# Shared tile's value product and O turn as whole-array products, its stores and remainder loads 64 rows outermost, and the first pair's q and k prepared head by head

## The chip, the cores and the metric

The kernel runs on one core of one Trainium2 chip. The metric is the device time in microseconds (us) of one execution. The kernel before takes 579.23 us (median of 3 runs, 577.52 to 580.37). The profiled execution's span, from its first to its last instruction, is some 1.8 us under the time measured for that execution; starts in the trace are counted from the start of the span.

## The reference, cut to what matters

```python
def _attn_ref(q, k, v, tau):                 # q, k, v: 8 batches, 8 heads, 576 rows, 64 columns
    scale = 1.0 / np.sqrt(q.shape[-1])
    scores = scale * np.matmul(q, k.transpose(0, 1, 3, 2))
    thresh = np.max(scores, axis=-1, keepdims=True) - tau
    scores = np.where(scores >= thresh, scores, -1000000000.0)
    ...                                      # softmax over what is left
    return np.matmul(attn, v)

def _moe_ref(x, w_in, w_out):                # x: 4608 x 512, w_in: 512 x 2048, w_out: 2048 x 512
    h = x @ w_in
    g = h - np.tanh(h)
    return g @ w_out
```

Attention's output, put back as 4608 rows of 512, is the MLP's input.

## The kernel before

It works on 32 pairs of heads, four pairs to a batch. A head has 576 = 4 x 128 + 64 rows, so a pair has nine score tiles of 128 rows: four for each head, and one *shared* tile that holds the 64 rows that are left over from both heads. I number pairs from 1, and follow the kernel by the start of each pair's shared value product. In pairs 1 to 4 there is no MLP work yet. The MLP weights are loaded piece by piece and cast by GpSimd from the start until pair 7. From pair 5 on, the MLP of the batch before is spread between the score tiles. Up to pair 8 the weights of the softmax are transposed on TensorE, later by DMA. kS is a copy of k with the halves swapped. After pair 32 the MLP of the last batch is left, and then that of all shared rows.

The parts that the change touches (cut; `...` marks cuts):

```python
    def split(p, t, fast=False):             # q or k as a sum of two fp16 parts
        ...                                  # fast (first pair): ScalarE and VectorE, all 576 columns at once
            nc.gpsimd.tensor_scalar(out=x, ...)
            nc.gpsimd.tensor_copy(out=hl[:, :, 0, :], in_=x)
            nc.gpsimd.tensor_tensor(out=hl[:, :, 1, :], ...)

    def attend(i):                           # value product
        ...
        if kd == "M":                        # the shared tile
            pt = pts.pop(i)
            for c in range(5):
                n = 64 if c == 4 else P
                for hh in range(2):          # half of the array's columns each
                    nc.tensor.matmul(
                        out=po[64 * hh : 64 * hh + 64, 4, :],
                        lhsT=pt[0:n, c * P + 64 * hh : c * P + 64 * hh + 64],
                        rhs=vb[0:n, hh, c, :], start=(c == 0), stop=(c == 4),
                    )
    ...
    def emit_x(p):                           # O turn: four whole-array transposes, then
        for hh in range(2):                  # the shared block, by quarters of the array
            s = slice(64 * hh, 64 * hh + 64)
            nc.tensor.matmul(out=ps[s, 512:576], lhsT=o[s, 4, 0, :], rhs=ident_bf[s, s], is_transpose=True, ...)
    ...
                rows = out.rearrange("(b s) n -> b s n", b=B)     # store of shared rows: batch outermost
                to = rows[2 * ms : 2 * ms + 2, MB:S, :]
    ...
            if s + AHEAD in w_when:          # every fourth score tile: one weight piece
                if loaded:
                    w_cast()                 # GpSimd, of the piece loaded four tiles ago
                piece = next(pieces, None)
                if piece:
                    w_load(piece)
```

In the traces GpSimd and the loads' queue each work in program order. Two places in these orders will matter: a weight cast stands on GpSimd in front of the next pair's split of k, and a weight load stands on its queue behind the two transfers of kS, a copy of k with the halves swapped, which must wait for VectorE's copy of the turned k (kS issued at 55.58 and 56.16 us, the load at 58.85).

Of the kernel before, what the change touches and what calls it, by code (L numbers as in the profile page):

```python
# [9 lines left out]
F32 = mybir.dt.float32  # L10
# [8 lines left out]
def kernel(  # L19
# [12 lines left out]
    P = 128  # L32
# [58 lines left out]
    for i in range(NM):  # L91
        zm = const.tile([P, 5 * P], BF16, name=f"zm{i}")
        nc.vector.memset(zm[:, S : 5 * P], -STEEP)
        zms.append(zm)

    pool = lambda name, bufs, **kw: ctx.enter_context(
        tc.tile_pool(name=name, bufs=bufs, **kw)
    )
# [18 lines left out]
    ps_y = pool("ps_y", 1, space=PSUM)  # L117

    ctx.enter_context(tc.manual_schedule())
    warm = const.tile([P, 1], F32, name="warm")  # L120
    nc.vector.memset(warm, 0.0)
    nc.scalar.activation(out=warm, in_=warm, func=ACT.Exp)


    raws = {}
# [3 lines left out]
    def load(p, t):  # L129
        b, h0 = p // HPAIR, 2 * (p % HPAIR)  # L130
        hs = slice(h0, h0 + 2)
        src = {"k": k, "q": q, "v": v}[t]
        eng = nc.scalar if p == 0 and t == "q" else nc.sync
        r = raws[p, t] = raw_pool.tile([P, 10, D], F32, name=f"{t}raw", tag=t)
        n = 8 if t == "v" else 10
        eng.dma_start(
            out=r[:, 0:n, :].rearrange("p (h c) d -> p h (c d)", h=2)[:, :, 0 : 4 * D],
            in_=src[b, hs, 0:512, :].rearrange("h (p c) d -> p h (c d)", c=4),
        )
        if t == "v":  # L140
            rem = src[b, hs, 512:S, :].rearrange("h s d -> s h d")
            eng.dma_start(out=r[0:64, 8:10, :], in_=rem)
            eng.dma_start(out=r[64:P, 8:10, :], in_=rem)
        else:
            eng.dma_start(out=r[:, 4, :], in_=src[b, hs, 512:S, :])

    hls = {}

    def split(p, t, fast=False):
        r = raws.pop((p, t))[:, 0:9, :]  # L150
        hl = hl_pool.tile([P, TPP, 2, D], FP16, name=f"{t}hl", tag=t)
        if fast:
            nc.scalar.mul(out=hl[:, :, 0, :], in_=r, mul=QKSC)
            nc.vector.scalar_tensor_tensor(
                out=hl[:, :, 1, :], in0=r, scalar=QKSC, in1=hl[:, :, 0, :],
                op0=ALU.mult, op1=ALU.subtract,
            )
        else:
            x = hl_pool.tile([P, TPP, D], F32, name="xs", tag="xs")
            nc.gpsimd.tensor_scalar(  # L160
                out=x, in0=r, scalar1=QKSC, scalar2=1.0, op0=ALU.mult, op1=ALU.mult
            )
            nc.gpsimd.tensor_copy(out=hl[:, :, 0, :], in_=x)
            nc.gpsimd.tensor_tensor(  # L164
                out=hl[:, :, 1, :], in0=x, in1=hl[:, :, 0, :], op=ALU.subtract
            )
        hls[p, t] = hl

    def split_v(p):
        r, vb = raws.pop((p, "v")), vbs[p % NV]  # L170
# [8 lines left out]

    mats = {}  # L180

    def turn(p, t):
        hl = hls.pop((p, t))
        ps = ps_big.tile([P, W], FP16, name=f"ps_{t}", tag="big")
        for c in range(TPP):
            nc.tensor.matmul(  # L186
                out=ps[:, c * P : (c + 1) * P],
                lhsT=hl[:, c, :, :].rearrange("p a d -> p (a d)"),
                rhs=ident_f16, is_transpose=True, start=True, stop=True,
            )  # L190
        m = qk_pool.tile([P, W], FP16, name=f"{t}T", tag=t)
        nc.vector.tensor_copy(out=m, in_=ps)  # L192
        mats[p, t] = m
        if t == "k" and p == 0:
            ps = ps_big.tile([P, W], FP16, name="ps_ks", tag="big")
            for c in range(TPP):
                for a in range(2):
                    nc.tensor.matmul(
                        out=ps[64 * a : 64 * a + 64, c * P : (c + 1) * P],
                        lhsT=hl[:, c, 1 - a, :],  # L200
                        rhs=ident_f16, is_transpose=True, start=True, stop=True,
                    )
            sw = qk_pool.tile([P, W], FP16, name="kS", tag="ks")
            nc.vector.tensor_copy(out=sw, in_=ps)
            mats[p, "ks"] = sw
        elif t == "k":
            sw = qk_pool.tile([P, W], FP16, name="kS", tag="ks")
            nc.sync.dma_start(out=sw[0:D, :], in_=m[D:P, :])
            nc.sync.dma_start(out=sw[D:P, :], in_=m[0:D, :])
            mats[p, "ks"] = sw  # L210


    MAIN = (slice(0, 512), slice(640, W))
# [101 lines left out]
    def attend(i):  # L315

        p, j = divmod(i, TPP)
        kd, vb = kind(j), vbs[p % NV]
        if kd == "A":
            return  # L320
        if j in (1, 6):
            ops[p, int(j > 4)] = ps_o.tile([P, 5, D + 1], F32, name="psO", tag="o")
        po = ops[p, int(j > 4)]
        if kd == "M":
            pt = pts.pop(i)
            for c in range(5):
                n = 64 if c == 4 else P
                for hh in range(2):
                    nc.tensor.matmul(  # L329
                        out=po[64 * hh : 64 * hh + 64, 4, :],  # L330
                        lhsT=pt[0:n, c * P + 64 * hh : c * P + 64 * hh + 64],
                        rhs=vb[0:n, hh, c, :], start=(c == 0), stop=(c == 4),
                    )
            return
        pt, hh = pts.pop(i), int(j > 4)

        for ab in range(2):
            blocks = [(4 * ab + ab + c, c) for c in range(4)]
            blocks.append((4, 4 + ab))
            for n, (blk, c) in enumerate(blocks):  # L340
                nc.tensor.matmul(  # L341
                    out=po[:, (j - 1 - 5 * hh) + ab, :],
                    lhsT=pt[:, blk * P : (blk + 1) * P], rhs=vb[:, hh, c, :],
                    start=(n == 0), stop=(n == 4),
                )
# [3 lines left out]
    def norm(p, hh):  # L349
        po = ops.pop((p, hh))  # L350
        if hh == 0:
            osb[p] = o_pool.tile([P, 5, 2, D], BF16, name="osb")
        n = 5 - hh
        rc = st_pool.tile([P, 5], F32, name="rc", tag="rc")
        nc.vector.reciprocal(out=rc[:, 0:n], in_=po[:, 0:n, D])
        nc.vector.tensor_tensor(
            out=osb[p][:, 0:n, hh, :], in0=po[:, 0:n, 0:D],
            in1=rc[:, 0:n].unsqueeze(2).to_broadcast([P, n, D]), op=ALU.mult,
        )

    xs = {}

    def emit_x(p):
        o = osb.pop(p)
        ps = ps_h.tile([P, S], BF16, name="psX", tag="h")
        for t in range(4):
            nc.tensor.matmul(
                out=ps[:, t * P : (t + 1) * P],
                lhsT=o[:, t, :, :].rearrange("p a d -> p (a d)"),
                rhs=ident_bf, is_transpose=True, start=True, stop=True,  # L370
            )
        for hh in range(2):
            s = slice(64 * hh, 64 * hh + 64)
            nc.tensor.matmul(
                out=ps[s, 512:576], lhsT=o[s, 4, 0, :], rhs=ident_bf[s, s],
                is_transpose=True, start=True, stop=True,
            )
        b = p // HPAIR
        if p % HPAIR == 0:
            xs[b] = x_pool.tile([P, DM_C, MB], BF16, name="xT")  # L380
        nc.vector.tensor_copy(out=xs[b][:, p % HPAIR, :], in_=ps[:, 0:512])
        nc.vector.tensor_copy(out=xR[:, p % HPAIR, b, :], in_=ps[:, 512:S])


    gs, stores = {}, []
# [29 lines left out]
    def project(m, ms, part, ps, last):  # L415
        for n in range(4 * part, 4 * part + 4):
            nc.tensor.matmul(  # L417
                out=ps, lhsT=gs[m][:, n, ms * P : (ms + 1) * P],
                rhs=w_out_sb[:, n, :], start=(n == 0), stop=(n == DF_C - 1),
            )  # L420
        if part == 3:
            yo = y_pool.tile([P, d_model], F32, name="yo")
            if last:
                nc.scalar.copy(out=yo, in_=ps)
            else:
                nc.vector.tensor_copy(out=yo, in_=ps)  # L426
            if m < B:
                rows = out[m * S : m * S + MB, :].rearrange("(p c) n -> c p n", c=4)
                to = rows[ms]
            else:  # L430
                rows = out.rearrange("(b s) n -> b s n", b=B)
                to = rows[2 * ms : 2 * ms + 2, MB:S, :]
            stores.append(lambda: nc.sync.dma_start(out=to, in_=yo))

    def layers(m, tail):

# [66 lines left out]
        for d, f in PREP[3 if p == 1 else 0 :]:  # L503
            plan.setdefault(first - d, []).append(lambda p=p, f=f: f(p))

    for t in ("k", "q", "v"):
        load(0, t)
    for t in ("k", "q"):
        split(0, t, fast=True)
    for t in ("k", "q"):  # L510
        turn(0, t)
    split_v(0)
    for t in ("k", "q", "v"):
        load(1, t)
# [8 lines left out]
    for s in range(-AHEAD, NTILE + LAG + 3):  # L523
# [7 lines left out]
            shift(s + AHEAD - 1)  # L531
        if 0 <= s + AHEAD < NTILE:
            scores(s + AHEAD)
        if 0 <= s + MASK < NTILE:
            kink(s + MASK)
        bend()
# [79 lines left out]
```

## Time and profile before

| | before |
|---|---|
| time, median (range) | 579.23 us (577.52 to 580.37) |
| span | 576.3 us |
| shared value product of pair 1, 5, 9, 32 | 28.78, 79.96, 138.57, 487.51 us |
| last pair's shared tile to the end | 88.76 us |
| distance of shared tiles deep in the middle | 15.65 us (13.56 for the first pair of a batch) |

The prediction below shows the lines for the bound, the start, the middle and the end. More will be needed: what VectorE pays for normalising one head's tile. The columns are line, engine, operation, tiles, shapes and count; then the busy sum and the mean in ns; then the idle time ahead:

```profile
L356 DVE TENSOR_TENSOR osb<-psO,rc 128x320 bf16<-128x320 f32 x32 | 15.7, 491 | 1.1
L356 DVE TENSOR_TENSOR osb<-psO,rc 128x256 bf16<-128x256 f32 x32 | 13.6, 424 | 1.1
```

Lines in order of time have start, length, operation, and in brackets the idle time before it with what ended it.

```profile
67.34 0.68 PE L186 MATMUL ps_k<-ident_f,khl 128*128 128x128 f16 x9 [1.05 <-POOL khl L164]
```

### The profile page before, as it was taken

What the parts mean: (1) busy time and instruction counts of PE and PEld (TensorE: products, weight loads), DVE (VectorE), ACT (ScalarE), POOL (GpSimd) and SP (SyncE); (2) the same over time, 40 slices, a digit from 0 to 9 for tenths busy, and PEclk for the clock granted to TensorE, in tenths of its full rate; (3) what the DMA queues carried; (4) which work ended last, traced back from release to release, by engine and by line L of the source; (5) the groups of instructions that cost most, each with busy time, mean ns of one, the idle gap of its engine ahead of it and who ended that gap; (6) DMA issues with size and microseconds to landing.
All of it is one profiled execution on the core that took longest, in us unless ns stands there. A gap on an engine that the chain in (4) does not pass through costs nothing.

```text
span 576.3 us, 13882 instructions
## 1 busy us (share of the span) xinstructions
PE 535.3 (93%) x5146; PEld 303.6 (53%) x5146; DVE 442.6 (77%) x1312; ACT 440.1 (76%) x634; POOL 215.6 (37%) x310
## 2 busy tenths in 40 slices
PE   3889899999999999998999999999999999999990
PEld 2566566665555555554555555555555555444440
DVE  3888888888988988888888888888889896444410
ACT  1889898898888898887898988888889888333400
POOL 6646683753433344444444343345333400000000
PEclk9999999999999999999999999999999999999996
DMA  6556755448889999779989999998999865110111
GB/s 180 170 170 175 211 171 160 138 109 176 176 180 183 180 197 197 173 179 185 174 192 182 186 196 178 188 203 189 179 185 176 184 128 120 38 38 36 38 45 46
DMA packets 186923, 89.48 MB, mean 155 GB/s; under 512 B 150632, under 2 KB 175208, under 8 KB 186856
## 3 DMA queue, kind: packets, MB, share of 16 engines
q1 hardware_dynamic: 186454, 88.31, 70.2%
q8 instruction: 40, 0.66, 0.5%
q10 hardware_dynamic: 402, 0.29, 0.2%
q14 instruction: 27, 0.22, 0.1%
HBM read 37.75 MB, written 9.44 MB: 82 GB/s over the span
## 4 chain that ended last, share of the span: by engine, by line
PE 75%; DMA 6%; ACT 6%; DVE 6%; POOL 2%; issue 1%; SPq 1%; ACTq 0%; POOLq 0%; DVEq 0%
PE psY L417 20%; PE psH L391 17%; PE psS L242 17%; PE psO L341 5%; PE ps_k L186 3%; PE psS L232 3%; ACT pT L302 3%; DVE sc L248 3%; DMA kS<-kT 2%; PE psHt L391 2%; PE psZ L293 2%; ACT z L274 2%; PE psO L329 2%; PE ps_q L186 2%; DMA out_dram<-yo 2%
## 5 line engine op out<-in xcount | busy, mean ns | idle before, releaser
L248 DVE TENSOR_SCALAR_CACHE_REDUCE sc<-psS 128x576 f32<-128x576 f32 x288 | 216.4, 751 | 24.4 <-PE psS L232 10.8
L274 ACT ACTIVATE z<-sc,nb 128x576 bf16<-128x576 f32 x256 | 195.5, 768 | 27.2 <-DVE nb L257 26.0
L417 PE MATMUL psY<-w_out_sb,g 128*128 128x512 bf16 x576 | 145.4, 379 | 0.0
L310 ACT ACTIVATE pT<-zT 128x1152 f16<-128x1152 bf16 (+1 forms) x120 | 127.9, 1066 | 11.6 <-DMA zT<-z 11.0
L391 PE MATMUL psH<-xT,w_in_sb 128*128 128x512 bf16 x480 | 123.4, 379 | 0.0
L242 PE MATMUL psS<-kT,qT 128*128 128x512 f16 (+1 forms) x512 | 105.7, 288 | 8.4 <-DVE nb L257 4.7
L242 PEld LDWEIGHTS <-qT 128*128 128x128 f16 x1024 | 74.8, 98 | 70.7 <-issue 12.4
L242 PE MATMUL psS<-kS,qT 128*128 128x512 f16 (+1 forms) x512 | 105.8, 289 | 2.7 <-DMA kS<-kT 2.6
L410 DVE SCALAR_TENSOR_TENSOR g<-th,psH 128x512 bf16<-128x512 f32 x128 | 87.3, 682 | 25.3 <-ACT th L404 25.1
L404 ACT ACTIVATE th<-psH 128x512 f32<-128x512 f32 x128 | 74.5, 582 | 18.6 <-PE psH L391 18.4
L160 POOL TENSOR_SCALAR xs<-kraw 128x576 f32<-128x576 f32 x31 | 20.8, 669 | 165.9 <-DMA kraw<-in_k_dram 120.3
L417 PEld LDWEIGHTS <-g 128*128 128x128 bf16 x576 | 49.6, 98 | 57.7 <-issue 2.5
L391 PEld LDWEIGHTS <-w_in_sb 128*128 128x128 bf16 x576 | 48.9, 98 | 54.2 <-issue 2.7
L341 PEld LDWEIGHTS <-pT 128*128 128x128 f16 x1280 | 55.6, 98 | 24.3 <-ACT pT L310 2.1
L341 PE MATMUL psO<-vb,pT 128*128 128x65 bf16 x1280 | 61.2, 193 | 0.6 <-ACT pT L310 0.6
L302 ACT ACTIVATE pT<-psZ 128x640 f16<-128x640 bf16 (+1 forms) x72 | 47.1, 654 | 10.6 <-PE psZ L293 10.5
L257 DVE TENSOR_SCALAR nb<-mx 128x1 f32<-128x1 f32 x288 | 42.5, 147 | 3.4
L164 POOL TENSOR_TENSOR qhl<-xs,qhl 128x576 f16<-128x576 f32 x31 | 39.7, 1279 | 2.6
L164 POOL TENSOR_TENSOR khl<-xs,khl 128x576 f16<-128x576 f32 x31 | 39.6, 1279 | 2.7
L274 ACT ACTIVATE zm<-sc,nb 128x576 bf16<-128x576 f32 x32 | 24.7, 773 | 17.3 <-DVE nb L257 17.1
L192 DVE COPY qT<-ps_q 128x1152 f16<-128x1152 f16 x32 | 24.2, 755 | 11.5 <-PE ps_q L186 11.5
L426 DVE COPY yo<-psY 128x512 f32<-128x512 f32 x30 | 20.7, 689 | 13.7 <-DMA out_dram<-yo 8.0
(60 smaller groups left out, 505.5 us busy)
## 6 DMA issues: line engine op xcount, KB each, us to landing
out_dram<-yo SPq DMA_DIRECT2D x36, 256.0 KB
kS<-kT SPq DMA_DIRECT2D x62, 144.0 KB
kraw<-in_k_dram SPq DMA_DIRECT2D x32, 256.0 KB
vraw<-in_v_dram SPq DMA_DIRECT2D x32, 256.0 KB
qraw<-in_q_dram SPq DMA_DIRECT2D x31, 256.0 KB
wt<-in_moe_w_in_dram SPq DMA_DIRECT2D x8, 512.0 KB
wt<-in_moe_w_out_dram SPq DMA_DIRECT2D x8, 512.0 KB
vraw<-in_v_dram SPq DMA_DIRECT2D x64, 32.0 KB
```

What stands on the lines that cost most here:

```text
L164: nc.gpsimd.tensor_tensor(out=hl[:, :, 1, :], in0=x, in1=hl[:, :, 0, :], op=ALU.subtract)
L242: nc.tensor.matmul(out=ps[:, dst], lhsT=lhs, rhs=kk[:, src], start=(n == 0), stop=(n == 1),)
L248: nc.vector.tensor_scalar(out=sc, in0=ps[:, lo : lo + S], scalar1=SC, scalar2=None, op0=ALU.mult, op1=ALU.max, accum_out=mx,)
L257: nc.vector.tensor_scalar(out=nb, in0=mx, scalar1=-1.0, scalar2=tau, op0=ALU.mult, op1=ALU.add)
L274: nc.scalar.activation(out=z, in_=sc, func=ACT.Prelu, bias=nb, scale=1.0, alpha=STEEP)
L302: nc.scalar.activation(out=pt[:, off * P : (off + n) * P], in_=ps[:, 0 : n * P], func=ACT.Exp)
L310: nc.scalar.activation(out=pt[:, 0 : n * P], in_=zts.pop(i)[:, 0:n, :], func=ACT.Exp)
L341: nc.tensor.matmul(out=po[:, (j - 1 - 5 * hh) + ab, :], lhsT=pt[:, blk * P : (blk + 1) * P], rhs=vb[:, hh, c, :], start=(n == 0), stop=(n ...
L391: nc.tensor.matmul(out=ps, lhsT=w_in_sb[:, c, n * P : (n + 1) * P], rhs=xs[m][:, c, :] if m < B else xR[:, c, :, :], start=(c == 0), stop= ...
L404: nc.scalar.activation(out=th, in_=ps, func=ACT.Tanh)
L410: nc.vector.scalar_tensor_tensor(out=gs[m][:, n, :], in0=th, scalar=-1.0, in1=ps, op0=ALU.mult, op1=ALU.add,)
L417: nc.tensor.matmul(out=ps, lhsT=gs[m][:, n, ms * P : (ms + 1) * P], rhs=w_out_sb[:, n, :], start=(n == 0), stop=(n == DF_C - 1),)
```

## The change

The shared value product becomes five whole-array matmuls of 130 columns, in which each row is multiplied with both heads' values; VectorE multiplies the unwanted half by zero (a mask, `own`), and the O turn becomes one whole-array product with `fold`, which adds rows s and s + 64. That avoids entering a divided array twice a pair. The shared rows are stored 64 rows at a time, and the remainder loads of k and q are put in another order, which should spread them over all 16 engines. The first pair's k and q are loaded, split and turned head by head, so that the first scores need only one head; ScalarE issues the loads of q ahead of its table load.

```diff
 if kd == "M":
     for c in range(5):
-        n = 64 if c == 4 else P
-        for hh in range(2):
-            nc.tensor.matmul(out=po[64 * hh : 64 * hh + 64, 4, :], lhsT=pt[0:n, ...], rhs=vb[0:n, hh, c, :], ...)
+        nc.tensor.matmul(out=po[:, 4:6, :], lhsT=pt[:, c * P : (c + 1) * P], rhs=vb[:, :, c, :], ...)
 ...
-    out=osb[p][:, 0:n, hh, :], in0=po[:, 0:n, 0:D], ...
+    out=osb[p][:, 0:4, hh, :], in0=po[:, 0:4, 0:D], ...
+if hh == 0:
+    nc.vector.scalar_tensor_tensor(
+        out=osb[p][:, 4, :, :], in0=po[:, 4:6, 0:D], scalar=rc[:, 4:5],
+        in1=own, op0=ALU.mult, op1=ALU.mult)
 ...
-for hh in range(2):
-    nc.tensor.matmul(out=ps[s, 512:576], lhsT=o[s, 4, 0, :], rhs=ident_bf[s, s], is_transpose=True, ...)
+nc.tensor.matmul(out=pf[:, 256:320], lhsT=o[:, 4, :, :].rearrange("p a d -> p (a d)"), rhs=fold, ...)
 ...
-    to = rows[2 * ms : 2 * ms + 2, MB:S, :]
+    for h in range(2):                      # b = 2 * ms + h
+        nc.sync.dma_start(out=out[b * S + MB : (b + 1) * S, :], in_=yo[64 * h : 64 * h + 64, :])
 ...
-    eng.dma_start(out=r[:, 4, :], in_=src[b, hs, 512:S, :])
+    rem = src[b, hs, 512:S, :].rearrange("h s d -> s h d")
+    eng.dma_start(out=r[:, 4, :], in_=rem)
 ...
-for t in ("k", "q"): split(0, t, fast=True)
-for t in ("k", "q"): turn(0, t)
+for t in ("k", "q"): split_first(t, 0)      # first head; the second follows among the first score tiles
+for t in ("k", "q", "ks"): turn_first(t, 0)
```

## The prediction

> **What bounds the kernel now.** The time to beat is 579.2 us (median); the profiled execution spans 576.3 us, and I reckon in the span and carry the difference over. I read the busy shares first, then the same by stage, then each stage's own limit.
>
> ```profile
> PE 535.3 (93%) x5146; PEld 303.6 (53%) x5146; DVE 442.6 (77%) x1312; ACT 440.1 (76%) x634; POOL 215.6 (37%) x310
> ...
> 15.00:75.00 60.00, 53.06 (x692) 36.41 (x691) 51.08 (x168) 52.75 (x84) 37.76 (x52) 1.00 0.62 181
> 130.00:242.00 112.00, 110.15 (x1076) 61.59 (x1075) 98.36 (x298) 97.42 (x133) 46.34 (x67) 1.00 0.90 182
> 242.00:298.00 56.00, 53.23 (x525) 29.77 (x524) 46.93 (x143) 46.77 (x66) 22.74 (x32) 1.00 0.99 183
> 298.00:465.00 167.00, 164.04 (x1607) 91.70 (x1606) 147.02 (x441) 144.67 (x198) 65.72 (x95) 1.00 0.92 184
> 495.00:545.00 50.00, 50.00 (x233) 22.68 (x232) 22.32 (x33) 19.07 (x32) 0.00 (x0) 1.00 0.10 38
> 553.00:575.00 22.00, 8.62 (x40) 3.72 (x38) 0.69 (x1) 1.17 (x2) 0.00 (x0) 0.80 0.13 48
> ```
>
> A row gives the stretch, then busy time of TensorE, its weight loads, VectorE, ScalarE and GpSimd, the clock, the DMA share, GB/s. There are five stages. 0 to 15 is the start. In 15 to 75 (four pairs, no MLP yet) nothing is full; ScalarE is at 0.88 with one buffer passed back and forth with TensorE, and I take this stage as ScalarE's. From 75 to 495 TensorE is without gaps but for some 10 us in 420: a TensorE microsecond saved there is a microsecond, as long as VectorE (0.88) and DMA (0.90 to 0.99) don't step in. In 495 to 545 it has no gap at all. In 553 to 575 TensorE is 0.39 busy, and nothing else is: that is a wait.
>
> The start: the first work waits for k, and TensorE for the splits.
>
> ```profile
> PE ps_k L186 <- DVE khl L154: 7.4, 1, 7.4
> ...
> ACT khl L153 <- DMA kraw<-in_k_dram: 3.6, 1, 3.6
> ```
>
> ScalarE begins the k split at 5.83 and TensorE the first scores at 12.33; the first row maximum on VectorE starts at 13.51 and the first exponential on ScalarE at 21.59.
>
> The middle, in order of time on TensorE (start, length, count at the end of the line):
>
> ```profile
> 241.10 0.39 PE L367 MATMUL psX<-ident_bf,osb 128*128 128x128 bf16 x4
> 241.42 0.22 PE L374 MATMUL psX<-ident_bf,osb 64*64 64x64 bf16 x2
> 241.57 0.42 PE L242 MATMUL psS<-kT,qT 128*128 128x512 f16 x2
> ...
> 243.42 1.03 PE L391 MATMUL psH<-xT,w_in_sb 128*128 128x512 bf16 x4
> 244.28 0.48 PE L341 MATMUL psO<-vb,pT 128*128 128x65 bf16 x10
> ...
> 245.31 1.04 PE L417 MATMUL psY<-w_out_sb,g 128*128 128x512 bf16 x4
> 246.28 0.47 PE L329 MATMUL psO<-vb,pT 128*64 128x65 bf16 x10
> 246.68 0.68 PE L186 MATMUL ps_k<-ident_f,khl 128*128 128x128 f16 x9
> 247.19 0.41 PE L242 MATMUL psS<-kT,qT 128*128 128x512 f16 x2
> ```
>
> Read the starts, not the lengths. Four 512-column matmuls before a whole-array group take 244.28-243.42 = 0.86 us; before the half-array L329 they take 246.28-245.31 = 0.97. Nine transposes take 247.19-246.68 = 0.51, so 0.056 each; four of them before L374 take 0.32 instead of 0.22. Each entry into a divided array thus costs 0.10 to 0.11 us.
>
> The end:
>
> ```profile
> 551.30 0.69 DVE L426 COPY yo<-psY 128x512 f32<-128x512 f32 x1 [3.00 <-PE psY L417]
> 554.80 0.58 ACT L424 COPY yo<-psY 128x512 f32<-128x512 f32 x1 [6.37 <-PE psY L417]
> 560.00 0.69 DVE L426 COPY yo<-psY 128x512 f32<-128x512 f32 x1 [8.01 <-DMA out_dram<-yo]
> 565.09 0.58 ACT L424 COPY yo<-psY 128x512 f32<-128x512 f32 x1 [9.71 <-DMA out_dram<-yo]
> ```
>
> The last two copies wait for a store to free their buffer, not for TensorE, whose last matmul (546.78 and 14.84 long) ends at 561.62. These are the four stores of the shared rows.
>
> **What the Trainium skill says.** *DMA: Bandwidth & Descriptors*, section "Why a DMA increments its semaphore by 16 and not by 1": a DMA runs on the largest number of engines up to 16 that divides the slowest dimension of both its sides, and on the lowest-numbered ones. The old shared-row store has the two batches outermost, so two engines. The trace agrees: DMA share 0.13 = 2.1 of 16, and 4 x 256 KB in 21 us, some 50 KB/us, where an ordinary 256 KB store issued at 548.46 has landed 2.0 us later. The old k and q remainder loads have the two heads outermost: two engines again, always the same ones. *TensorEngine Tiling (Array Packing)*, "Key Properties": changing the tiling mode drains TensorE. The trace shows the 0.10 us above. *TensorE: Matmul & The Clock Gate*, "Back-to-back issue gap": N/2.4 + 2.5 ns when warm. The trace agrees (0.86/4 = 0.215 at 512, 0.056 at 128). *ScalarE: Activation LUTs*, "What ACT_TABLE_LOAD costs": 186 ns + 0.833 ns per element; here 576 elements take 682 ns against 666.
>
> **The change part by part.**
>
> *Value product of the shared tile.* Before: ten half-array matmuls, 246.68-246.28 = 0.40, and the entry, 0.11: 0.51, less nothing at the exit worth counting (0.01). After: five whole-array matmuls of 130 columns; 130/2.4+2.5 = 57 ns each (an estimate by the formula that held above): 0.28. Gain 0.22 us a pair.
>
> *O turn of the shared tile.* Before: 241.57-241.42 = 0.15 plus the entry 0.10, 0.25. After: one matmul of 64 columns, 0.03. Gain 0.22 us a pair.
>
> Both in the 28 pairs under the MLP: 28 x 0.44 = 12.3 us at most. What doesn't count: each batch's first pair has its O turn in the steps without MLP work, where TensorE waits for VectorE anyway (7 x 0.22 = 1.5 us). Some coupling is lost too, because VectorE gains an instruction: the normalisation of 128x320 (491 ns) becomes 128x256 (424) and one over 128 elements, which the slope between those two rows, 1.05 ns per element, puts at 290. So +0.22 us a pair, 6 us over the 28 pairs on an engine with 12% idle. Its share goes from 0.88 to 0.92 while TensorE's work shrinks by 3%. I take 10% off for that: (12.3-1.5) x 0.9 = 9.7 us. In the four pairs of the first stage, set by ScalarE, I count nothing.
>
> *Remainder loads over 16 engines.* No work removed, but the two crowded engines are relieved. One stall in the chain comes from a late landing: kS, issued 263.89, took 5.81 us, and TensorE waited 1.9. I count 1 us.
>
> *Stores of 64 rows.* Now 64 is outermost, 16 engines, two issues per tile (0.33 us each as the ordinary stores of the tail). No buffer wait remains: the last copy starts at 561.7, ends 562.3; first store 562.35, second 562.75, landed 2.0 later, 564.75; from the last landing to the end of the span it was 1.0 us before. End at 565.8 instead of 576.3: gain 10.5 us.
>
> *First pair by head.* k's first head and the remainder are issued first, and the remainder no longer queues on two engines. ScalarE now issues three q loads ahead of its 1.28 us table load, so its split can begin at about 4.4 instead of 5.83. Then 320 elements instead of 576: ScalarE 0.47, VectorE about 0.49, ten transposes (cold) 1.3, ten half-array ones 0.65, copies; first scores at about 7.7, first row maximum near 9 instead of 13.5. The second head is not removed but inserted: two splits (2 x 0.41 on ScalarE, about as much on VectorE), 16 transposes after the third score tile, and three ScalarE copies of 512 (0.6 each) which stand in ScalarE's order ahead of the first z. That puts the first z at about 13.7 (14.50 before); six of them at 0.78 bring the first exponential to 18.4 instead of 21.59. Since ScalarE paces the next stage, I count that: 3 us.
>
> Sum: 9.7 + 1 + 10.5 + 3 = 24.2 us.
>
> **The rivals.** (1) DMA becomes the bound of the middle: its share is 0.90 to 0.99, and the stretch at 0.99 is also the one where TensorE lost 2.8 of 56 us. For it: a pair shortened by 3% asks for 3% more. Against: 0.90 x 15.65 us (the distance of shared tiles) is 14.1, under the 15.2 aimed at, and the change unloads the fullest engines. If true, the middle gives 4 us and the total is about 561. (2) VectorE takes over: +0.22 us a pair in its chain of maxima. For: TensorE's rare waits are mostly for VectorE's nb. Against: 0.92 is not full. If true, the middle gives 6, total 559. (3) The start gives back its lead: the four pairs after it wait for k and q of pair 1 or weight loads on GpSimd (16.5 us of waits for weights), or for ScalarE's inserted copies. Then 0 to 1 us instead of 3: 557. (4) Better than I think: no loss in the middle, the stall gone altogether, 4.5 us at the start: 549.
>
> **Range and chances.** 579.2 - 24.2 = 555.0 us. The end is the surest term (9.5 to 11), the middle the widest (6 to 13), the start 0.5 to 4.5, the stall 0 to 2. Combined not all at one edge: 549 to 561. Faster by 2% needs 11.6 us, which the end nearly gives alone: 0.96; within 2% 0.035; slower 0.005.
>
> **What would show it.** The last copy at TensorE's last matmul without a store ahead of it, and about 4 us from there to the end. L329's and L374's successors as 128*128 groups of five and one, with the 0.97 and 0.32 back at 0.86 and 0.22. Shared tiles of pairs deep in the middle 15.2 us apart instead of 15.65. First exponential near 18.4. VectorE's new instruction near 290 ns. I am wrong about the end if the 64-row stores still crawl at 50 KB/us; about the middle if the starts of groups move as said but pairs stay 15.65 apart, with a new wait in front of the scores.

## More of the kernel before

```profile
63.52 1.04 POOL L473 CAST w_in_sb<-wt 128x1024 bf16<-128x1024 f32 x1 [4.65 <-DMA wt<-in_moe_w_in_dram]
64.53 0.67 POOL L160 TENSOR_SCALAR xs<-kraw 128x576 f32<-128x576 f32 x1
65.26 0.66 POOL L163 CAST khl<-xs 128x576 f16<-128x576 f32 x1
66.01 1.27 POOL L164 TENSOR_TENSOR khl<-xs,khl 128x576 f16<-128x576 f32 x1
```

GpSimd is idle for 4.65 us, with pair 5's k long there: the cast in front of it waits for a weight load.

## The result, and the profile after

The changed kernel takes 560.00 us (median of 4 runs, 559.74 to 560.57), the kernel before in the same rounds 578.87. Ratios here are the mean time of one kernel's runs over that of the other's of the same rounds, so not quite the ratio of the quoted medians: 0.9675, with a 95% interval of 0.9649 to 0.9700. That lies inside the predicted range, 5 us above its middle and 1 us below its upper end. The profiled span is 558.2 us: 18.1 us less, where the terms added up to 24.2.

The busy shares of the changed kernel:

```profile
PE 524.3 (94%) x4954; PEld 303.1 (54%) x4954; DVE 445.6 (80%) x1349; ACT 442.3 (79%) x640; POOL 214.8 (38%) x310
```

TensorE has 192 matmuls and 11.0 us less work, VectorE 3.0 us more.

To see where the time went, I took the start of each pair's shared value product in both traces. The lead of the changed kernel is 2.3 us at pair 1 and 2.8 at pair 3; it is *minus* 0.1 at pair 5, 0.3 at pair 9, 7.6 at pair 32 and 18.1 at the end. So the end gave 10.5 us (88.76 to 78.23), the size predicted; the start's lead was there and was lost; and the middle gave 7.7 where I had counted 10.7 (with the stall).

**The end.** In order of time:

```profile
546.92 0.59 ACT L477 COPY yo<-psY 128x512 f32<-128x512 f32 x1 [6.36 <-PE psY L470]
550.33 0.69 DVE L479 COPY yo<-psY 128x512 f32<-128x512 f32 x1 [6.22 <-PE psY L470]
553.83 0.59 ACT L477 COPY yo<-psY 128x512 f32<-128x512 f32 x1 [6.32 <-PE psY L470]
```

The last copies wait for TensorE and no longer for a store; the span ends 4.4 us after the last one's start.

**The micro costs** on TensorE:

```profile
239.68 0.39 PE L421 MATMUL psX<-ident_bf,osb 128*128 128x128 bf16 x4
239.90 0.19 PE L427 MATMUL psX<-fold,osb 128*128 128x64 bf16 x1
239.93 0.41 PE L292 MATMUL psS<-kT,qT 128*128 128x512 f16 x2
...
243.66 1.04 PE L470 MATMUL psY<-w_out_sb,g 128*128 128x512 bf16 x4
244.54 0.45 PE L378 MATMUL psO<-vb,pT 128*128 128x130 bf16 x5
244.83 0.67 PE L221 MATMUL ps_k<-ident_f,khl 128*128 128x128 f16 x9
```

From start to start: four transposes take 0.22 us (0.32 before), the fold 0.03 (0.15), the MLP group ahead of the value product 0.88 (0.97), the value product 0.29 (0.40). The sum falls from 1.84 to 1.42 us a pair, by 0.42: the estimate was 0.44.

**VectorE:**

```profile
L404 DVE TENSOR_TENSOR osb<-psO,rc 128x256 bf16<-128x256 f32 x64 | 27.2, 425 | 2.2
L409 DVE SCALAR_TENSOR_TENSOR osb<-psO,rc,own 128x128 bf16<-128x128 f32 x32 | 10.9, 342 | 0.0
```

The new instruction takes 342 ns, not 290. With the shorter normalisation that is 425 + 342 - 491 = 0.28 us a pair more, by the lengths. VectorE's instructions overlap, though: from the start of that normalisation to the start of what follows it was 0.41 us in one pair of the kernel before (247.01 to 247.42) and is 0.60 in the changed one (245.28 to 245.88), only 0.19 more. That is part of why VectorE's busy time grows by 3.0 us and not by 32 x 0.28 = 9.

**Where the start's lead went.** GpSimd ahead of pair 5, then TensorE there, then the stretch around it (columns as in the prediction), first of the kernel before, then of the changed one:

```profile
62.84 1.04 POOL L531 CAST w_in_sb<-wt 128x1024 bf16<-128x1024 f32 x1 [5.54 <-DMA wt<-in_moe_w_in_dram]
63.85 0.67 POOL L179 TENSOR_SCALAR xs<-kraw 128x576 f32<-128x576 f32 x1
64.58 0.66 POOL L182 CAST khl<-xs 128x576 f16<-128x576 f32 x1
65.33 1.27 POOL L183 TENSOR_TENSOR khl<-xs,khl 128x576 f16<-128x576 f32 x1
```

```profile
63.93 0.45 PE L378 MATMUL psO<-vb,pT 128*128 128x130 bf16 x5
66.66 1.14 PE L221 MATMUL ps_k<-ident_f,khl 128*128 128x128 f16 x9 [2.27 <-POOL khl L183]
67.59 0.63 PE L292 MATMUL psS<-kT,qT 128*128 128x512 f16 x1
```

```profile
60.00:75.00 15.00, 12.74 (x174) 9.00 (x173) 12.34 (x42) 13.02 (x22) 10.90 (x15) 1.00 0.70 212
```

```profile
60.00:75.00 15.00, 11.99 (x148) 8.51 (x146) 10.85 (x37) 11.02 (x19) 11.59 (x15) 0.89 0.64 196
```

The weight load hardly gains: it is issued 1.60 us earlier (57.25 instead of 58.85), but its cast starts only 0.68 us earlier than before, and TensorE waits 2.27 us instead of 1.05. What follows the wait runs at a lower granted clock: nine transposes take 67.59 - 66.66 = 0.93 us instead of 0.51, and the mean clock of the stretch is 0.89 instead of 1.00 (0.50 from 66.25 to 69.66 us, 1.00 on both sides). From pair 4 to pair 5 the changed kernel takes 16.15 us, the one before 14.14. Of these 2.0 us the longer wait is 1.2; I estimate the rest, 0.8, as the lower clock. Another 0.9 us goes one pair earlier, at a first wait for the split of 1.31 us (52.50), which the kernel before doesn't have. The fall of the clock belongs to this execution: the mean clock of its whole span is 0.997, that of the other three runs 0.999, 1.0 and 1.0, where 3.41 us at half would take off 0.003; they took 560.04, 560.57 and 559.74 us all the same.

**The middle.** Deep in it, the distance of shared tiles falls from 15.65 to 15.22 us for a batch's second and fourth pair, to 15.42 for the third, and from 13.56 to 13.29 for the first. I call what a pair takes above these regular distances a stall. From pair 9 to pair 32 the regular part gives 7.9 us, while stalls grow from 3.1 to 3.7 us together: the one at pair 18 shrinks from 2.23 to 0.65, but pair 14 gets 1.2, pair 25 0.8 and pair 31 0.6. From pair 5 to pair 9 the gain is only 0.4.

### The profile page after: what moved, and what is told of

Same layout as the page of the kernel before. It is cut to its first block, busy times and chain, and to the rows that moved or that the text cites. A ratio compares the mean times of both kernels' runs of the same rounds, so it can differ in the third digit from the quotient of the medians. Undisturbed runs are those within 1.5% of the kernel's fastest.

```text
span 558.2 us, 13552 instructions
## 1 busy us (share of the span) xinstructions
PE 524.3 (94%) x4954; PEld 303.1 (54%) x4954; DVE 445.6 (80%) x1349; ACT 442.3 (79%) x640; POOL 214.8 (38%) x310
## 4 chain that ended last, share of the span: by engine, by line
PE 63%; DVE 15%; ACT 9%; DMA 7%; issue 3%; SPq 1%; POOL 1%; ACTq 0%; DVEq 0%; POOLq 0%
PE psY L470 18%; PE psH L444 15%; PE psS L292 13%; DVE sc L298 6%; PE psO L389 4%; ACT z L324 3%; DVE g L463 3%; ACT pT L352 3%; PE psS L282 3%; DMA zT<-z 2%; PE psHt L444 2%; DMA kraw<-in_k_dram 2%; PE ps_q L221 2%; PE ps_k L221 2%; PE psZ L343 2%
## 5 line engine op out<-in xcount | busy, mean ns | idle before, releaser
L292 PE MATMUL psS<-kS,qT 128*128 128x512 f16 x496 | 101.8, 287 | 0.2 <-DMA kS<-kT 0.2
L352 ACT ACTIVATE pT<-psZ 128x640 f16<-128x640 bf16 (+1 forms) x72 | 47.2, 656 | 11.6 <-PE psZ L343 11.1
L221 PE MATMUL ps_k<-ident_f,khl 128*128 128x128 f16 x288 | 22.2, 223 | 10.6 <-DVE khl L195 6.8
L343 PE MATMUL psZ<-ident_bf,z 128*128 128x128 bf16 x288 | 26.7, 220 | 4.4 <-ACT pT L352 4.3
```

Source lines behind the costliest of these rows:

```text
L221: nc.tensor.matmul(out=out, lhsT=lhsT, rhs=rhs, is_transpose=True, start=True, stop=True)
L292: nc.tensor.matmul(out=ps[:, dst], lhsT=lhs, rhs=kk[:, src], start=(n == 0), stop=(n == 1),)
L352: nc.scalar.activation(out=pt[:, off * P : (off + n) * P], in_=ps[:, 0 : n * P], func=ACT.Exp)
```

## The experiments

Eleven kernels ran, in three groups. Each group shared one chip with runs of the kernel before; the median of those is given. (The first two groups ran on the same chip and share all but one of these runs.) Leads are read from the profiled run of each kernel as above: us by which it is ahead of the kernel before at a pair's shared tile, negative where it is behind.

| kernel | time, us | ratio | pair 1 | pair 5 | pair 9 | pair 32 | end |
|---|---|---|---|---|---|---|---|
| changed kernel | 560.00 | 0.9675 | 2.3 | -0.1 | 0.3 | 7.6 | 18.1 |
| stores alone | 568.07 | 0.9821 | 0.0 | 0.5 | 0.5 | 0.0 | 10.1 |
| whole array alone | 571.54 | 0.9881 | -0.5 | -1.9 | -1.5 | 6.6 | 6.7 |
| start and loads alone | 574.45 | 0.9928 | 3.0 | 2.4 | 2.4 | 4.0 | 3.9 |
| changed, late casts | 555.31 | 0.9600 | 2.5 | 3.6 | 4.0 | 11.4 | 22.0 |
| changed, mask left out | 556.95 | 0.9638 | 2.6 | 2.7 | 3.8 | 12.3 | 22.8 |
| changed, mask twice | 567.87 | 0.9804 | 3.0 | 2.2 | 0.9 | 2.4 | 12.9 |
| before, late casts | 576.79 | 0.9966 | -0.8 | 1.0 | 1.0 | 0.0 | 0.1 |
| before, remainder loads alone | 575.53 | 0.9942 | 1.1 | -0.3 | -0.4 | 2.2 | 2.1 |
| whole array, late casts | 570.88 | 0.9865 | 0.4 | 2.4 | 2.8 | 7.0 | 7.2 |
| changed, early loads | 556.27 | 0.9612 | 1.5 | 2.5 | 2.9 | 10.0 | 20.6 |
| changed, late casts, copy on ScalarE | 559.42 | 0.9676 | 2.7 | 2.5 | 0.4 | 8.4 | 18.9 |

How far can a lead be trusted? Up to pair 32 the program of stores alone is that of the kernel before, and yet its leads there lie between -0.1 and 0.7 us, its stall at pair 10 is 0.7 us longer, and its stalls from pair 9 to 32 sum to 3.6 us instead of 3.1. So a single stall, a sum of stalls or a lead that differs by less than some 0.7 us in one trace says little. The stretch from pair 5 to pair 9 is far steadier: 58.61 to 58.63 us in all five kernels with the old shared tile, and 58.20 to 58.22 in five with the new one.

My theory after the result: the start's lead is lost because GpSimd has a weight cast in front of pair 5's split, and the middle falls short for another reason, either VectorE's new work or waits that TensorE doesn't set. The rival: the parts are simply worth less than I had counted.

### First group: each part alone, and the casts later

The median of the kernel before was 579.17 us.

**Stores alone.** The kernel before with the change's two 64-row stores for each shared tile.

```diff
-    to = rows[2 * ms : 2 * ms + 2, MB:S, :]
+    two stores of 64 rows, as in the change
```

> The kernel before with nothing changed but the shared rows' stores, each cut in two stores of 64 rows. Theory (the old store ran on two engines): the buffer waits of 8.0 and 9.7 us ahead of the last two copies vanish, everything earlier is as before, and the time falls by 10 to 11 us, 578.9 to about 568.4. Rival (the end was slow for another reason, or part of the end's gain in the changed kernel came from the work ahead of it): less than 8 us.

It took 568.07 us (566.87 to 570.02), 0.9821 (0.9783 to 0.9859): 11.1 us less, 10.1 in the spans. Its last copy:

```profile
561.72 0.59 ACT L424 COPY yo<-psY 128x512 f32<-128x512 f32 x1 [6.32 <-PE psY L417]
```

It waits for TensorE alone. The term of the end is confirmed by itself: from the last shared tile to the end it is 78.65 us, 10.1 less than before. The other 0.4 us of the changed kernel's 10.5 came with the other parts.

**Whole array alone.** The value product, the mask and the O turn of the change, and nothing else of it.

```diff
+    the change's own and fold, its value product, normalisation and O turn, in the kernel before
```

> The kernel before with nothing changed but the shared tile's value product, normalisation and O turn in whole-array mode. Theory: TensorE gains 0.44 us in every pair, but it is worth 0.43 only where nothing else is waited for, 0.2 to 0.3 in two pairs of each four, and next to nothing in the first nine pairs, so the gain is 5.5 to 8.5 us (about 571.9). My prediction's term alone said 9.7 us (569). Rival (VectorE's extra instruction eats it): under 4 us.

It took 571.54 us (571.32 to 572.85), 0.9881 (0.9854 to 0.9908), a gain of 7.6, within the 5.5 to 8.5 expected. Its trace shows that this isn't a steady 7.6: it *loses* 1.9 us up to pair 5, where TensorE waits twice for GpSimd's split (1.42 us at 55.74 and 1.89 at 69.53), then gains 8.4 up to pair 32.

**Start and loads alone.** The first pair by head, and the remainder loads over all engines.

```diff
+    load_first, split_first, turn_first and the 64-row order of the remainder loads, in the kernel before
```

> The kernel before with the first pair prepared by head, and with the k and q remainder loads spread, but with the old shared tile and the old stores. Theory: the first shared tile's value product comes 2.3 us earlier (28.8 to 26.5), the lead stands at 2.5 to 2.8 us up to the third pair and is gone by the fifth (near 80.0 as before), because the k split of the fifth pair stands on GpSimd behind a weight cast that waits for its load; only a late kS landing (about 2 us) may be gained later. Total gain 0 to 2.5 us. Rival (the start's lead was kept and the middle lost it): 3 us or more, with the fifth shared tile near 77.3.

It took 574.45 us (574.24 to 575.10), 0.9928 (0.9903 to 0.9954): 4.7 us gained. My expectation was wrong. The lead of 3.0 at pair 1 is still 2.4 at pair 5, and the stall at pair 18 shrinks from 2.23 to 0.5 us. TensorE waits once for the split, 1.72 us, 0.67 more than in the kernel before, and just that is lost. So the start's lead isn't lost by itself. The whole-array part loses at pair 5 too; so, in one trace, do the remainder loads alone (below). Alone, the three parts gain 11.1 + 7.6 + 4.7 = 23.4 us, close to the predicted 24.2; together 18.9. The sum fails in how they meet, and that speaks against the rival.

**Changed, late casts.** Each weight piece is cast four score tiles later than in the changed kernel, when its load has had twice the time.

```diff
-    w_when = [4 * i + 3 for i in range(17)]
+    w_when = [4 * i + 3 for i in range(18)]
 ...
-                if loaded:
+                if len(loaded) == 2 or (loaded and s + AHEAD >= 4 * 16 + 3):
                     w_cast()
```

> The changed kernel with one thing moved: each weight cast on GpSimd comes one slot (four tiles) later, so that its load has had twice the time. Theory (the weight cast that waits for its load holds up the k split of the fifth pair, TensorE stands 2.3 us and its clock is halved): the wait before the fifth pair's k turn shrinks under 0.5 us, no stretch before 80 us has a granted clock under 0.95, the fifth shared tile comes at about 77.3 instead of 80.1, and the time falls by 2 to 3.5 us to 557.3. Rival (the DMA bandwidth or ScalarE sets the pace of the first 80 us): fifth shared tile still near 80, time within 0.8 us of 560.0.

It took 555.31 us (553.17 to 558.57), 0.9600 (0.9556 to 0.9644), so it beats both kernels, and by more than the 2 to 3.5 us expected. The same stretch:

```profile
60.00:75.00 15.00, 13.29 (x175) 9.42 (x174) 13.31 (x47) 14.37 (x24) 12.35 (x18) 1.00 0.82 256
```

The clock is back at 1.00, TensorE has no wait for the split left, and its nine transposes of k take place at 63.73 instead of 66.66. The lead at pair 5 is 3.6 instead of -0.1. The theory for the start is confirmed; and the gain of all parts, 579.17 - 555.31 = 23.9, is again about the sum of the parts alone. What it doesn't change is the middle: from pair 5 to pair 32 it gains 7.8 us, the changed kernel 7.7.

### Second group: VectorE's new instruction, and two controls

The median of the kernel before was 579.02 us.

**Mask left out.** VectorE as before the change (one normalisation of five blocks), TensorE as after it. The shared rows come out wrong.

```diff
-    out=osb[p][:, 0:4, hh, :], in0=po[:, 0:4, 0:D], ...
-    if hh == 0: nc.vector.scalar_tensor_tensor(...)
+    out=osb[p][:, 0:n, hh, :], in0=po[:, 0:n, 0:D], ...
 ...
-    lhsT=o[:, 4, :, :].rearrange("p a d -> p (a d)"),
+    lhsT=o.rearrange("p c a d -> p (c a d)")[:, 448:576],
```

> The changed kernel without VectorE's new instruction (the old single normalisation of five blocks comes back, wrong result on purpose: one head's 64 remainder rows come out wrong), so TensorE as in the changed kernel and VectorE as before it. Theory A (the middle falls short of 12.3 us because VectorE has 0.28 us more to do in each pair): most of the 3 us come back, time 556.5 to 557.5 us, and the distance of shared tiles in positions 1 and 3 of a batch stays 15.2 while positions 0 and 2 reach it too (13.2 and 15.2). Theory B (VectorE's work has slack; the middle falls short because of waits for buffers and first-of-batch pairs that TensorE does not set): within 1 us of the changed kernel, 559 to 561.

It took 556.95 us (555.26 to 559.41), 0.9638 (0.9601 to 0.9675): 3 us less than the changed kernel's 560.00, as theory A had it in size, though the two intervals overlap, and its slowest run comes within 0.4 us of the changed kernel's fastest. The profiled run was the fastest of the four; its span is 4.7 us shorter. But not in the way that A said. The regular distances deep in the middle are the same as with the mask: 15.22, 15.42, 15.22, 13.30. There the mask was free. What came back was the lead at pair 5 (2.7), 0.8 us between pairs 5 and 9, and 1.2 us of stalls after pair 9. The first of these is the split's waits, which got shorter (2.3 us instead of 3.6, 1.8 at the longest), and the granted clock, which stays at 1.00 in this execution. It isn't VectorE's work as such, as the next run shows.

**Mask twice.** The same instruction issued twice, with a right result.

```diff
+    nc.vector.scalar_tensor_tensor(...)     # the same one again
```

> The changed kernel with VectorE's new instruction emitted twice (right result), so 0.34 us a pair more on VectorE and nothing else. Theory A (VectorE sets the middle): at least half of 32 x 0.34 = 11 us appears, 565 us or more. Theory B (slack): less than 2 us, 560 to 562.

It took 567.87 us (565.16 to 568.51), 0.9804 (0.9770 to 0.9838): 7.9 us more than the changed kernel. (The profiled run, at 565.16, was the fastest of its four.) The regular distances become 15.57, 15.80, 15.57 and 13.67: each 0.35 to 0.38 us longer, which is the whole of the second instruction. So the first mask took up what slack VectorE's chain had deep in the middle, and nothing of a second one is hidden. TensorE's own waits between 80 and 138 us (pairs 5 to 9) rise in the same order. Here are the first lines of what TensorE waited for there: total us, times, longest; before, changed, mask left out, mask twice:

```profile
PE psS L242 <- DVE nb L257: 0.7, 3, 0.4
```

```profile
PE psS L292 <- DVE nb L307: 1.7, 5, 0.5
```

```profile
PE psS L292 <- DVE nb L307: 0.9, 3, 0.4
```

```profile
PE psS L292 <- DVE nb L307: 3.5, 5, 1.0
```

The waits for VectorE's row maxima grow with the mask, and in this stage even one mask costs: from pair 5 to pair 9 the four kernels take 58.61, 58.22, 57.45 and 59.96 us. Without the mask the whole-array form would have given 1.2 us here; with it it gives 0.4. With two masks the lead at pair 5 is 2.2 us, so more work on VectorE does not by itself cause the loss at the split. How the queues happen to stand to each other seems to decide it; that is not shown.

**Before, late casts.** The control for the late casts.

```diff
+    the two lines of the late casts, in the kernel before
```

> The kernel before with only each weight cast one slot (four score tiles) later. Theory (the late cast pays by removing TensorE's wait for GpSimd's split in front of the fifth pair, which is 1.1 us here against 2.3 in the changed kernel): 0.5 to 1.5 us faster, 577.5 to 578.7. Rival (later casts help by themselves everywhere, and what late casts gave the changed kernel has nothing to do with the changed start): 4 us or more faster, 575 or less.

It took 576.79 us (576.72 to 578.02), 0.9966 (0.9937 to 0.9996): 2.2 us less by the medians, a little more than expected and far from the rival's 4. Its trace is ahead by 1.0 at pair 5, just the wait of 1.05 us, and has lost that again at pair 22, in a stall of 1.2 us; the profiled run was the slowest of its four. So late casts pay little without the change's other parts.

**Before, remainder loads alone.**

```diff
-    eng.dma_start(out=r[:, 4, :], in_=src[b, hs, 512:S, :])
+    eng.dma_start(out=r[:, 4, :], in_=src[b, hs, 512:S, :].rearrange("h s d -> s h d"))
+    the order of the transposes that goes with it
```

> The kernel before with only the k and q remainder loads spread over all engines (64 rows outermost) and the transposes' order that this needs. Theory (two crowded queues cause the late kS at the 18th pair, 2.2 us too long there): that pair becomes 15.7 to 16.2 us long instead of 17.9, and the start is a little earlier as k's remainder lands sooner; 1.5 to 3 us faster, 576 to 577.5. Rival (the stall is any late transfer under a DMA share of 0.99): the pair stays over 17 us or the stall turns up elsewhere, and the time is within 1 us of before.

It took 575.53 us (574.23 to 576.08), 0.9942 (0.9914 to 0.9970). Pair 18 takes 15.65 us: its stall is gone. In the kernel before it was this wait:

```profile
PE psS L242 <- DMA kS<-kT: 1.9, 1, 1.9
```

So in this arrangement the old order of the remainder loads did hold kS up, and the new one is worth about the 2 us of that stall. I had counted 1. That two crowded engines are the reason fits, but isn't shown by itself: whole array alone has the old loads and only 0.09 us of stall at pair 18.

This trace also loses at pair 5: the lead of 1.3 at pair 4 becomes -0.3. The wait for the split is 1.50 us, 0.45 more than in the kernel before, and the granted clock is 0.50 from 66.87 to 70.28 us; I estimate the rest of the 1.66 us lost, 1.2, as the clock's. The other three runs have a mean clock of 0.990 or 0.991 instead of 0.986, so not this fall.

### Third group: the loop at the split, and VectorE relieved

The median of the kernel before was 578.18 us; five rounds.

**Whole array, late casts.**

```diff
+    the two lines of the late casts, in the kernel with the whole-array part alone
```

> The kernel before with the whole-array part alone and each weight cast one slot later. The whole-array part alone gained 7.6 us and had lost 1.9 us by the fifth pair, where TensorE waited for GpSimd's split of k. Theory (that loss is the wait behind the weight cast, and the whole-array part is worth its 9 to 10 us without it): fifth shared tile at 79 to 80 instead of 81.83, time 568.5 to 570.0 us, 9 to 10.5 us under the kernel before. Rival (the part is worth 7.6 us whatever GpSimd does): 571 to 572.

It took 570.88 us (569.11 to 571.69), 0.9865 (0.9840 to 0.9889). By the time the rival is right: this part gains 7.3 us here, no more than without the late casts. By the trace both halves of the story hold: the pair-5 loss is gone (lead 2.4 instead of -1.9, more than expected), but from pair 9 on 6.8 us of stalls stand where the whole array alone had 3.0: 1.3 at pair 14, 1.75 at pair 18, 1.2 at pair 31. This kernel still has the crowded remainder loads. So a lead won early can be lost to stalls later, and I cannot say of one stall what it would be in another arrangement.

**Changed, early loads.** Casts where the change has them, but each load issued two score tiles earlier, in front of the kS transfers on the queue.

```diff
-            if s + AHEAD in w_when:
-                if loaded:
-                    w_cast()
+            if s + AHEAD in w_when and loaded and s + AHEAD > 3:
+                w_cast()
+            if s + AHEAD + 2 in w_when:
                 piece = next(pieces, None)
                 if piece:
                     w_load(piece)
```

> The changed kernel with the casts where they were and each weight load issued two score tiles earlier, so that it no longer stands on its queue behind the two kS transfers, which wait for VectorE's copy of k. Theory (the cast in front of the split is late because its load is issued late, in a loop of cast, split, turn, kS transfer and next load): GpSimd's waits for weight loads between 30 and 72 us fall from 16.9 us to under 8, TensorE's wait for the split (3.6) to under 1, fifth shared tile at 76 to 77.5, time 555 to 557. Rival (the load itself is slow among the other transfers, wherever it is issued; only a cast behind the split helps): fifth tile still at 79 or later, 559 to 560.5.

It took 556.27 us (554.60 to 557.50), 0.9612 (0.9589 to 0.9636). GpSimd's waits for weights between 30 and 72 us of this kernel:

```profile
POOL w_in_sb L531 <- DMA wt<-in_moe_w_in_dram: 6.5, 1, 6.5
POOL w_out_sb L531 <- DMA wt<-in_moe_w_out_dram: 2.6, 1, 2.6
```

The waits fall from 16.9 us to 9.1 (I had expected under 8), TensorE's wait for the split is gone, and pair 5's tile is at 77.47, at the edge of what was expected. Part of the lead is paid at the start (1.5 instead of 2.3 us at pair 1). Relieving the queue gives the same as relieving GpSimd. The loss was thus a loop through four queues: the cast waits for its load, the split for the cast, TensorE for the split, VectorE's copy of k for TensorE, kS for the copy, and the next load stands behind kS.

**Changed, late casts, copy on ScalarE.** One try to beat the late casts: 0.215 us a pair taken off VectorE.

```diff
-        nc.vector.tensor_copy(out=xR[:, p % HPAIR, b, :], in_=pf[:, 256:320])
+        nc.scalar.copy(out=xR[:, p % HPAIR, b, :], in_=pf[:, 256:320])
```

> The changed kernel with the late casts (555.3 us) and the copy of the shared rows' O turn on ScalarE instead of VectorE: 0.215 us a pair less on VectorE, about 0.25 more on ScalarE. If VectorE's new work costs the 2 us that the kernel without it gained between the fifth and the last pair, and ScalarE has room (0.88 of the middle): 1 to 2 us faster than 555.3, 553.3 to 554.3. If ScalarE has no room, or its order delays the copy and thereby the buffer for the hidden layer: same or slower, 555 to 560.

It took 559.42 us (558.11 to 560.90), 0.9676 (0.9653 to 0.9699): 4 us slower than the late casts alone. From pair 5 to pair 9 it takes 60.77 us instead of 58.21, so 2.6 of the 3.0 us between the two traces lie in that one stage, where ScalarE is busy 0.90 of the time (49.73 of 55 us, in the kernel before). From pair 9 to pair 32 it gained 0.7, all of it in stalls. ScalarE has no room for it in pairs 5 to 8; no other engine was tried.

## Why the prediction was right or wrong, point by point

The prediction was right in kind, and its range held by 1 us. Its sum was 6.1 us too large by the spans. (Rival 4's 549 doesn't add up either: its terms give 555.0 - 2.6 - 0.9 - 1.5 = 550.)

| term | predicted, us | measured, us |
|---|---|---|
| end | 10.5 | 10.5 |
| whole array, pairs 9 to 32, regular part | 8.3 | 7.9 |
| whole array, pairs 5 to 9 | 1.4 | 0.4 |
| stalls | 1 | -0.6 |
| start | 3 | -0.1 |
| sum | 24.2 | 18.1 |

(The 9.7 us of the middle are split here by its own rule: four pairs of which one is a batch's first, (4 x 0.44 - 0.22) x 0.9 = 1.4, and the rest.)

- *The end* was right in the term and in the mechanism, and stores alone show 10.1 of the 10.5 us. That the term came out at 10.5 to the digit is partly luck, as 0.4 us of it are not the stores'.
- *The micro costs* were right: 0.42 against 0.44 us a pair. The second and fourth pairs of a batch gain all of it, 15.65 to 15.22. The third gains half, with or without the mask. In the one such pair that I looked at (225 us), TensorE's hidden-layer group, which follows the O turn directly there, starts 0.2 us late; that its buffer is freed too late is my reading, not shown.
- *VectorE* was named as a rival and dismissed with "0.92 is not full". Deep in the middle that held, by a hair: one mask cost nothing, the second all of itself. In pairs 5 to 8 it did not hold. The step that failed there is "From 75 to 495 TensorE is without gaps": it took one sentence for two stages. In pairs 5 to 8 TensorE's 53.47 of 55 us stand beside a ScalarE at 0.90, and what TensorE saves there is passed on only in part. The mask's 342 ns instead of 290 are the smaller error.
- *The stall* of kS shrank from 2.23 to 0.65 us, the remainder loads alone remove it, and it was under-sized (2 us instead of 1). The reason given is likely but not shown: with the old loads it is 0.09 us in whole array alone and 1.75 with the late casts. And other stalls took its place, so that their sum, 3.7 us instead of 3.1, changed by no more than one trace wanders. Pair 14's, which I followed, comes down to a late transposed tile:

```profile
197.85 0.69 DVE L463 SCALAR_TENSOR_TENSOR g<-th,psH 128x512 bf16<-128x512 f32 x1 [2.10 <-ACT th L457]
...
198.52 0.75 DVE L298 TENSOR_SCALAR_CACHE_REDUCE sc<-psS 128x576 f32<-128x576 f32 x1
...
199.33 0.41 PE L292 MATMUL psS<-kT,qT 128*128 128x512 f16 x2 [0.92 <-DVE sc L298]
```

  VectorE waits 2.10 us for ScalarE's tanh, which stands behind an exponential that waits for its DMA transpose, and TensorE then waits 0.92 us for VectorE. So rival 1 (DMA) was right in a small way: not as a bound, but as late landings. Why they fall where they do is not settled; whole array with late casts had 6.8 us of them, the kernel with the mask twice only 1.4 (in the fastest of its four runs).
- *The start* failed as a net term. Its first lines in the changed kernel are:

```profile
5.38 0.47 ACT L194 ACTIVATE khl<-kraw 128x320 f16<-128x320 f32 x1 [1.42 <-DMA kraw<-in_k_dram]
...
9.73 0.76 DVE L298 TENSOR_SCALAR_CACHE_REDUCE sc<-psS 128x576 f32<-128x576 f32 x1 [0.73 <-PE psS L292]
...
19.34 0.60 ACT L352 ACTIVATE pT<-psZ 128x512 f16<-128x512 bf16 x1 [0.87 <-PE psZ L343]
```

  The split begins at 5.38 us instead of 4.4, since it still waits 1.42 us for k to land. The first row maximum comes at 9.73 ("near 9"), the first exponential at 19.34 instead of 18.4, and the lead of 2.3 to 2.8 us was close to the 3 predicted. But it was then lost at the weight cast. That is rival 3, "The start gives back its lead", which had the right engine: it named the "weight loads on GpSimd (16.5 us of waits for weights)" and I gave it too little weight. What I had missed is that the kernel before already showed a wait of 1.05 us at that spot: a queue that is already late sets the pace there, and an earlier start can lengthen the wait instead of paying off. How much of it is lost differs: the changed start alone keeps 2.4 of its 3.0 us. The late casts and the early loads, from two sides, show that this wait was what ate the lead. In the single parts the waits account for the loss: the whole-array form alone waits twice (1.42 and 1.89 us), the changed start alone once (1.72), where the kernel before waits 1.05. What stays open is why the earlier of the two waits appears in some arrangements only, and what makes the clock fall in some executions.

The step to name is thus the start's term, and in the middle the term of pairs 5 to 8.

## What to carry to other kernels

Before you count a lead at the start of a kernel, look downstream for the first wait that is set by another queue: a transfer that is issued behind something, a cast in front of something else in the same engine's program order. Moving that piece of work by one slot, two changed lines here, was worth 4.7 us by the medians of two groups (4.3 by the ratios), as much as the new start and loads by themselves. And where an engine has slack, ask how much: here one added instruction of 0.34 us was free in the steady part and the second cost all of itself, while in a neighbouring stage even the first was not free.

## What the Trainium skill lacked or had wrong

- *TensorEngine Tiling (Array Packing)*, "Key Properties", says that a change of the tiling mode drains TensorE, but gives no figure. Here the entry cost 0.09 to 0.10 us each time (0.97 to 0.88 us for a group of four matmuls, 0.32 to 0.22 for four transposes), some 0.2 us a pair.
- *TensorE: Matmul & The Clock Gate*, "What's actually happening", gives an idle window of about 3.4 us for the fall of the clock. Here the clock was 0.50 from 66.25 to 69.66 us, though TensorE was busy for 1.55 of the 3.41 us before that and had waited for only 1.86 us when the clock fell; nine transposes then took 0.93 instead of 0.51 us. Nor does the length of one wait decide it: after 1.50 us the clock fell (remainder loads alone), after 1.89 us it did not (whole array alone). The page's Part 4 says that the full clock doesn't engage for transposes; here transposes among other matmuls run 0.056 us apart, the spacing of the full clock.
- *VectorE: DVE Perf Modes*, "The TRN2 errata — SBUF-src ops pay a fixed extra latency per instruction", has one row for every VectorE operation from PSUM to SBUF, which makes 258 ns for 128 elements (my estimate, at one element a cycle), and no figure for the scalar-tensor-tensor. It takes 342 ns here, against an estimate of 290 from the tensor-tensor rows.
- No page that I read warns of the loop by which a cast on GpSimd, placed ahead of another pair's work, paces TensorE: 16.9 us of GpSimd's waits for weight loads between 30 and 72 us, and 3.6 us of TensorE's for the split.
